# A fused attention, MLP and mixer kernel: later landings in its planner, layer-norm sums as two float32r products, new tables of positions

## Chip, cores and metric

The kernel runs on one core of one Trainium2 chip. The time is that of one execution on the device, in microseconds (us); before the change it is 1037.3 us, the median of three runs (1037.26 to 1037.39). The engines are TensorE (PE in the profile, its weight loads PEld), VectorE (DVE), ScalarE (ACT), GpSimd (POOL) and SyncE (SP), which here only issues transfers.

## The reference

Attention with a causal mask and a bias from a running sum, then a layer norm with an MLP, then a mixing over the sequence with a second MLP:

```python
scores = scale * q @ k.T ; bias = -(cum_i - cum_j)        # per batch and head, S = 576, D = 64
attn = softmax(where(causal, -1e9, scores + min(bias, 0))) ; x = attn @ v   # heads joined: (4, 576, 512)
mu = mean(x, -1) ; var = mean((x - mu) ** 2, -1)
xn = (x - mu) / sqrt(var + 1e-6) * g_ln
x = x + relu(xn @ w_ch1) @ w_ch2                          # 512 -> 2048 -> 512
u = x + (x.T @ U @ V).T                                   # rank 32, over the sequence
out = u + relu(u @ w2_ch1) @ w2_ch2
```

## The kernel before

Four batches of 576 tokens are cut into blocks. In the first layer A0 to A3 are the first 256 tokens of each batch and B0 to B3 the other 320; in the second layer C0 to C3 are the first 512 tokens and T0 the last 64 of all four. Most products are exact to about float32 by splitting both operands into a float32r part and a float32r rest and adding three products (`xh` with `w` high, `xh` with `w` low, `xl` with `w` high, lines 1396 to 1398, 1453 to 1455); C blocks use a scheme with seven sums (lines 1309 to 1311 and 1347 to 1349).

A0 and A1 are normalised token by token (`layer_norm_tok`), with no product. A2, A3 and B0 to B3 are held with features on the partitions, so their mean and variance need a sum over partitions: `ln_sum` adds the four tiles on DVE or POOL into `into` and multiplies the result by a matrix `ones` of 1/512, as one float32 product (line 967). `layer_norm` calls it twice for each block, so there are 12 such sums. What it makes, `xh` and `xl`, is read by the block's first MLP product.

No order is written by hand. Every piece of work is an operation with a priority, a cost per engine it may run on, its reads and writes. `Plan.issue` plans all of them up to five times (`PASSES`), engine by engine, and emits the instructions in the planned order of the shortest plan. So each engine's queue is fixed when the program is built, and each engine takes its queue strictly in order. A transfer (`load`, line 376, loads and stores alike) is taken by the planner to be there 1.5 us (`hop`) after its planned end, plus `lag`. `AT` gives the interval of steps over which a block's attention is spread, `LN` the step at which its layer norm is given, `HEAD` by how much the operations of the start are put ahead of their latest planned time. `split` makes a high part (ACT or DVE) and a rest (DVE or POOL).

Three places matter below. The values of a B block's attention come through two buffers `xs` (line 661), are split into `v` (lines 382, 386) and read much later by line 867; scores come from PE lines 765, 769 and 747 and leave PSUM by DVE lines 773 and 752. In T0 the weights come through two buffers `pB` of 1 MB each (line 1511, `w1_load`), and the second layer's other weights through `w` (line 1517). `t_mix` for T0 loads `t` (line 1161) before its products on line 1244.

Of the kernel before, what the change touches and what calls it, by code (L numbers as in the profile page):

```python
# [10 lines left out]
F32R = mybir.dt.float32r  # L11
I32 = mybir.dt.int32
U32 = mybir.dt.uint32
AF = mybir.ActivationFunctionType
# [17 lines left out]
LAST = ("C0", "C1", "C2", "T0", "C3")  # L32
W2SLOTS = 12

AT = {"A2": (1, 3), "A3": (1, 33), "B0": (26, 49), "B1": (50, 65), "B2": (67, 83), "B3": (83, 100)}
LN = {"A2": 9, "A3": 33, "B0": 62, "B1": 66, "B2": 84, "B3": 102}
W0 = (1, 14)
HEAD = {-100: -1, -50: 127, 1.5: 61, 4.5: 18, -4: 1, -3: -8}
W1 = (16, 60, 59)
PASSES = 4  # L40
AHEAD = 1500


def f(ap):
    return ap.bitcast(F32)


def mm_cost(n):
    return max(106.7, n / 2.4) + 13.3
# [39 lines left out]
class Plan:  # L89
# [196 lines left out]
    def issue(self, warm):  # L286
# [9 lines left out]
        for _ in range(PASSES):  # L296
            prio = self.latest(order, end)
            for o in self.ops:
                prio[o.seq] -= 1e3 * HEAD.get(o.prio, HEAD.get(o.prio + 500, 0))
            use = {e: [0.0] * NW for e in price}  # L300
# [35 lines left out]
def mha_ffn_mixer_ffn(ctx: ExitStack, tc, qkv_p, qkv_a, qkv_b, s, g, w1, w2, U, V, out):  # L336
    nc = tc.nc
    P = Plan(nc)
# [20 lines left out]
    def psum():  # L359
        return P.buf("ps", [128, 512])  # L360
# [6 lines left out]
    def act(prio, n, fn, reads, writes, fixed=94):  # L367
        P.op(prio, {"act": (fixed + 0.8333 * n, fn)}, reads, writes)

    def pe(prio, cost, fn, reads, writes, hold=()):  # L370
        return P.op(prio, {"pe": (cost, fn)}, reads, writes, hold=hold)
# [2 lines left out]
        return 4 * max(n / 2.4, 53.3) + 2.5  # L374

    def load(prio, nbytes, fn, reads, writes, gate=None, rate=350.0, lag=0):
        P.op(prio, {"sp": (475, fn)}, reads, writes, nbytes, gate, rate=rate, lag=lag)

    def copy(prio, n, out, a, reads, writes, psum=False, soft=0.0, slow=False):
        P.op(prio, {  # L380
# [10 lines left out]
    def split(prio, n, hi, lo, src, reads, wh, wl, psum=False, soft=0.0, slow=False):  # L391
        copy(prio, n, hi, src, reads, wh, psum, soft, slow)
        tt(prio, n, lo, src, lambda: f(hi()), ALU.subtract, list(reads) + list(wh), wl, psum, soft)


    def fixed(name, shape, dtype=F32):
        return P.fixed(const.tile(shape, dtype, name=name))

    ident = fixed("ident", [128, 128])
    ones = fixed("ones", [128, 128])  # L400
    eps = fixed("eps", [128, 1])
    odd = fixed("odd", [128, 1])
    g_sb = fixed("g_sb", [128, KT])
    small = fixed("small", [128, 4])
# [14 lines left out]
    PRO = -1e6  # L419

    def setup():
# [14 lines left out]
            dve(PRO, 1, lambda a=a, z=z: nc.vector.memset(odd[a:a + R], z), [], [(odd, "y%d" % a)])  # L436
        dve(PRO, 128, lambda: nc.vector.memset(ones.tile, 1.0 / DM), [], [ones], 0.521)
        P.op(PRO, {"pool": (600, lambda: nc.gpsimd.memset(causal.tile, 0.0))}, [], [causal])
        for y in range(4):
            act(PRO, R, lambda y=y: nc.scalar.activation(sel[R * y:R * (y + 1)], ident[R * y:R * (y + 1), R * y:R * (y + 1)], AF.Copy),  # L440
                [ident, table], [(sel, "y%d" % y)])
# [131 lines left out]
    def w2_ahead(m, gate):  # L573
        prio = NS0 + m - 8
        raw, t = w_raw(prio, 1, m, 1, gate, AHEAD), psum()
        f64_to_f32(prio, 512, lambda: t.tile, lambda: raw.tile, t, raw, psum=True)
# [3 lines left out]
    def w1_ahead(p, gate):  # L580
        prio, dr = NS0 + 2 * p - 9, w1_dr[p]
        raws, ts = [], []
        for z in range(2):
            raw, t = w_raw(prio, 1, 2 * p + z, 0, gate, AHEAD), psum()
            f64_to_f32(prio, 512, lambda t=t: t.tile, lambda raw=raw: raw.tile, t, raw, psum=True)
# [31 lines left out]
    class Pair:  # L617
# [94 lines left out]
        def bias(self, prio, tick, gate):  # L712
# [5 lines left out]
            for y in range(2):  # L718
                load(prio, 256 * S, lambda t=t, y=y: nc.sync.dma_start(
                    t[64 * y:64 * (y + 1)], cum_dr[idx + y:idx + y + 1].to_broadcast([64, S])), [cum_dr], [(t, "y%d" % y)], gate, 260.0, AHEAD // 2)  # L720
                d = lambda y=y: t[64 * y:64 * (y + 1), 512:S]
# [239 lines left out]
    def ln_sum(prio, n, srcs, reads, into):  # L961

        for k in range(1, KT):
            tt(prio, n, lambda: into[:, :n], srcs[0] if k == 1 else lambda: into[:, :n], srcs[k], ALU.add,
               (reads[0] if k == 1 else [into]) + reads[k], [into])
        ps = psum()
        pe(prio - 500, 4 * mm_cost(n), lambda: nc.tensor.matmul(ps[:, :n], ones.tile, into[:, :n], start=True, stop=True), [ones, into], [ps])
        return ps

    def layer_norm(prio, b, blk):  # L970
# [105 lines left out]
    def mix_prep_v(prio, gate):  # L1076
        hi, lo = (P.buf("t", [128, S], F32R) for _ in range(2))
        n = S // 2
        for c0 in (0, n):
            raw, v = P.buf("wr", [128, 1024]), psum()  # L1080
            for z in range(4):
                load(prio, RANK * 8 * n, lambda z=z, c0=c0, raw=raw: nc.sync.dma_start(
                    raw[RANK * z:RANK * (z + 1), :2 * n].bitcast(U32), V[:, c0:c0 + n].bitcast(U32)), [], [(raw, "z%d" % z)], gate, lag=AHEAD)
            f64_to_f32(prio, n, lambda v=v: v[:, :n], lambda raw=raw: raw[:, :2 * n], v, raw, (None, None), psum=True)
# [390 lines left out]
    def put(pos, fn):  # L1475
        plan[int(pos * 4)].append((pos, fn))
# [45 lines left out]
    for st in range(NS0, NS, 2):  # L1522
        _, _, blk, m = steps[st]
# [25 lines left out]
    put(start1 - 12, lambda p, g: mix_prep_v(p, g))  # L1549
    for x in AT:  # L1550
        b, blk = int(x[1]), x[0]
        if x not in FULL:
            for p, pr in enumerate(pairs_of[b, blk]):
                put(max(0, AT[x][0] - 6 + p), lambda p, g, pr=pr: pr.bounce(p, g))
        spread(attn_items(b, blk), *AT[x])
        put(LN[x], lambda p, g, b=b, blk=blk: layer_norm(p, b, blk))
    for (l, b, blk), p in final.items():
# [14 lines left out]


    setup()
    for _, fn in attn_items(0, "A"):
        fn(-100, None)
# [76 lines left out]
```

## Time and profile before

| | |
|---|---|
| median of three runs | 1037.3 us |
| the profiled execution's own time | 1036.19 us |
| its span, first to last instruction | 1034.4 us |
| PE busy | 1017.1 us (98%) |
| DVE busy | 694.6 us (67%) |
| ACT busy | 470.2 us (45%) |
| POOL busy | 138.5 us (13%) |
| DMA engines, main queue | 69.6% |
| granted TensorE clock, mean | 1.000 |

Engine times are sums of what each engine was busy. Products follow each other in a pipeline and are recorded from their start to a modelled end, so a product's recorded duration (308 ns in the mean for the costliest line) is longer than the distance to the next one, and two neighbours overlap. A wait shorter than that overlap doesn't appear as idle time. The 1.8 us between span and time lie outside the first and last instruction.

### The profile page before, as it was taken

The numbers are of one execution on the slowest core, as the hardware profiler recorded it, in microseconds if no ns is written. First come the engines' busy times: TensorE is split into PE (matmuls) and PEld (weight loads), VectorE is DVE, ScalarE is ACT, GpSimd is POOL, SyncE is SP. The second block draws the span as 40 slices with busy tenths as digits, with TensorE's granted clock in tenths as the row PEclk, the third lists the DMA queues.
The fourth block names the chain that finished last, engine by engine and source line by source line (L and its number), as shares of the span: only waits on it lengthen the run. The fifth ranks groups of instructions, "written<-read, shape, count | busy, mean of one in ns | idle before, by whom it ended". The sixth has DMA issues, their size and how long they took to land.

```text
span 1034.4 us, 19312 instructions
## 1 busy us (share of the span) xinstructions
PE 1017.1 (98%) x7110; PEld 938.8 (91%) x7110; DVE 694.6 (67%) x1760; ACT 470.2 (45%) x1104; POOL 138.5 (13%) x288
## 2 busy tenths in 40 slices
PE   8999999999999999989999999999999999999998
PEld 7888888999999999979999999898999899899897
DVE  7999989866988878678754428547446645517444
ACT  6889877755856556557543314312111211112110
POOL 0021333511620222032100000001001000001000
PEclk9999999999999999999999999999999999999999
DMA  8999984668656976595475799981763576487851
GB/s 296 342 339 344 335 310 145 212 228 295 215 165 201 305 245 218 181 315 184 128 286 205 248 394 358 348 321 46 266 217 106 198 240 191 143 287 235 316 172 42
DMA packets 99231, 248.80 MB, mean 241 GB/s; under 512 B 16416, under 2 KB 47392, under 8 KB 94528
## 3 DMA queue, kind: packets, MB, share of 16 engines
q1 hardware_dynamic: 98464, 246.97, 69.6%
q8 instruction: 56, 0.92, 0.4%
q10 hardware_dynamic: 672, 0.59, 0.2%
q14 instruction: 39, 0.32, 0.1%
HBM read 193.97 MB, written 62.99 MB: 248 GB/s over the span
## 4 chain that ended last, share of the span: by engine, by line
PE 77%; DVE 5%; DMA 2%; ACT 2%; issue 1%; SPq 0%; DVEq 0%; POOL 0%; ACTq 0%; POOLq 0%
PE ps L1396 6%; PE ps L1398 5%; PE ps L1397 5%; PE ps L1309 5%; PE ps L1311 5%; PE ps L1310 5%; PE ps L867 4%; PE acc L1453 4%; PE acc L1454 4%; PE acc L1455 4%; PE ps L823 3%; PE acc L1347 3%; PE acc L1349 3%; PE acc L1348 3%; PE ps L1347 3%; PE ps L1348 3%
## 5 line engine op out<-in xcount | busy, mean ns | idle before, releaser
L1396 PE MATMUL ps<-xh,w 128*128 128x256 f32 (+1 forms) x512 | 157.8, 308 | 1.8 <-DVE pB L386 0.9
L1398 PE MATMUL ps<-xl,w 128*128 128x256 f32 (+1 forms) x512 | 151.3, 295 | 0.0
L1397 PE MATMUL ps<-xh,w 128*128 128x256 f32 (+1 forms) x512 | 151.2, 295 | 0.0
L1403 DVE SCALAR_TENSOR_TENSOR hl<-ps,hh 128x256 fp32r<-128x256 f32 (+1 forms) x144 | 64.5, 449 | 94.4 <-ACT hh L1402 94.0
L1402 ACT ACTIVATE hh<-ps 128x256 fp32r<-128x256 f32 (+1 forms) x144 | 58.2, 404 | 119.1 <-PE ps L1398 118.4
L1396 PEld LDWEIGHTS ps<-xh,w 128*128 128x128 f32 x512 | 96.7, 189 | 9.1 <-DVE pB L386 1.6
L1397 PEld LDWEIGHTS ps<-xh,w 128*128 128x128 f32 x512 | 96.8, 189 | 2.2
L1453 PE MATMUL acc<-hh,w 128*128 128x256 f32 (+1 forms) x320 | 97.3, 304 | 0.0
L1398 PEld LDWEIGHTS ps<-xl,w 128*128 128x128 f32 x512 | 96.6, 189 | 0.0
L1454 PE MATMUL acc<-hh,w 128*128 128x256 f32 (+1 forms) x320 | 93.8, 293 | 0.0
L1455 PE MATMUL acc<-hl,w 128*128 128x256 f32 (+1 forms) x320 | 93.8, 293 | 0.0
L1269 ACT ACTIVATE w<-hl 128x256 fp32r<-128x256 f32 x83 | 34.1, 418 | 124.7 <-DVE hl L1289 124.5
L783 ACT ACTIVATE t<-t,mx 128x384 f32<-128x384 f32 (+4 forms) x112 | 68.9, 617 | 47.0 <-DVE mx L773 39.2
L1289 DVE TENSOR_TENSOR hh<-ps,hh 128x256 f32<-128x256 f32 x64 | 27.1, 423 | 77.7 <-ACT hh L381 76.1
L1289 DVE TENSOR_TENSOR hl<-ps,hh 128x256 f32<-128x256 f32 x128 | 48.6, 419 | 44.9 <-PE ps L1311 43.7
L381 ACT ACTIVATE hh<-ps 128x256 f32<-128x256 f32 x31 | 12.0, 386 | 113.9 <-PE ps L1311 113.7
L386 DVE TENSOR_TENSOR pB<-ps,pB 128x384 fp32r<-128x384 f32 (+2 forms) x112 | 60.0, 569 | 5.2 <-ACT pB L381 4.7
L773 DVE CUSTOM_DVE_ANT_0 t<-ps,causal 128x128 f32<-128x128 f32 (+3 forms) x128 | 56.9, 484 | 8.5 <-PE ps L769 8.1
L1453 PEld LDWEIGHTS acc<-hh,w 128*128 128x128 f32 x320 | 60.7, 190 | 1.5 <-issue 1.0
L1454 PEld LDWEIGHTS acc<-hh,w 128*128 128x128 f32 x320 | 60.7, 190 | 0.5
L1455 PEld LDWEIGHTS acc<-hl,w 128*128 128x128 f32 x320 | 60.6, 190 | 0.0
L1295 DVE SCALAR_TENSOR_TENSOR w<-hl,w 128x256 fp32r<-128x256 f32 x128 | 52.3, 426 | 6.6 <-ACT w L1269 5.7
(258 smaller groups left out, 2894.8 us busy)
## 6 DMA issues: line engine op xcount, KB each, us to landing
w<-w_dr SPq DMA_DIRECT2D x112, 512.0 KB, 7.3
pB<-w_dr SPq DMA_DIRECT2D x36, 1024.0 KB, 5.4
qk<-w_dr SPq DMA_DIRECT2D x28, 768.0 KB, 5.2
w_dr<-w SPq DMA_DIRECT2D x32, 512.0 KB, 6.0
w_dr<-wr SPq DMA_DIRECT2D x32, 512.0 KB, 4.8
wr<-w1a SPq DMA_DIRECT2D x16, 512.0 KB, 6.3
wr<-w2a SPq DMA_DIRECT2D x16, 512.0 KB, 6.2
wr<-w1b SPq DMA_DIRECT2D x16, 512.0 KB, 6.5
```

Source lines behind the costliest of these rows:

```text
L386: alts = {"dve": (68 + 1.042 * n, lambda: nc.vector.tensor_tensor(out=out(), in0=a(), in1=b(), op=op))}
L783: act(prio, K, lambda t=t, mx=mx, o=o, K=K, x=x, y=nt * z + x: nc.scalar.activation(t[:, o:o + K], t[:, o:o + K], AF.Exp, bias=mx[:, (1 if ...
L1289: dve(st - 1000, 256, lambda: nc.vector.tensor_tensor(out=d.tile, in0=region(r), in1=a.tile, op=ALU.add), [p, a], [d])
L1347: nc.tensor.matmul(aa[z].tile, w[:, 0, sl], h[:, 0], start=first, stop=False)
L1348: nc.tensor.matmul(aa[z].tile, w[:, 1, sl], h[:, 0], start=False, stop=False)
L1396: nc.tensor.matmul(ps[:, :n], lhs(k, 0), xh[:, k, :n], start=k == 0, stop=False)
L1397: nc.tensor.matmul(ps[:, :n], lhs(k, 1), xh[:, k, :n], start=False, stop=False)
L1398: nc.tensor.matmul(ps[:, :n], lhs(k, 0), xl[:, k, :n], start=False, stop=k == KT - 1)
L1403: dve(st - 1000, n, lambda: nc.vector.scalar_tensor_tensor(out=hl[:, :n], in0=ps[:, :n], scalar=0.0, in1=f(hh[:, :n]), op0=ALU.max, op1=AL ...
L1453: nc.tensor.matmul(a, w[:, 0, sl], hh[:, :n], start=new, stop=False)
L1454: nc.tensor.matmul(a, w[:, 1, sl], hh[:, :n], start=False, stop=False)
L1455: nc.tensor.matmul(a, w[:, 0, sl], hl[:, :n], start=False, stop=last and (z == 1 or blk == "B"))
```

## The change

- `load` lets the planner take every transfer whose priority is above 0 to land at least `LATE` = 1000 ns later than before (an operation that had a larger `lag` keeps it). Only the planned order depends on it; no wait and no transfer is added by it.
- `ln_sum` splits the sum `into` into two float32r tiles from the pool `ls` and multiplies each by a float32r copy `mean_w` of `ones`; one cast at the start makes that copy. In place of one float32 product there are two float32r products, and before them one cast and one subtraction.
- `AT`, `LN` and `HEAD` have new numbers.

```diff
-AT = {"A2": (1, 3), "A3": (1, 33), "B0": (26, 49), "B1": (50, 65), "B2": (67, 83), "B3": (83, 100)}
-LN = {"A2": 9, "A3": 33, "B0": 62, "B1": 66, "B2": 84, "B3": 102}
+AT = {"A2": (1, 3), "A3": (1, 32), "B0": (26, 49), "B1": (50, 65), "B2": (67, 84), "B3": (85, 100)}
+LN = {"A2": 9, "A3": 32, "B0": 62, "B1": 66, "B2": 85, "B3": 102}
-HEAD = {-100: -1, -50: 127, 1.5: 61, 4.5: 18, -4: 1, -3: -8}
+HEAD = {-100: -1, -50: 117, 1.5: 41, 4.5: 16, -4: 1, -3: -8}
+LATE = 1000
...
-        P.op(prio, {"sp": (475, fn)}, reads, writes, nbytes, gate, rate=rate, lag=lag)
+        P.op(prio, {"sp": (475, fn)}, reads, writes, nbytes, gate, rate=rate, lag=max(lag, LATE if prio > 0 else 0))
...
+    mean_w = fixed("mean_w", [128, 128], F32R)
...
+        act(PRO + 1, 128, lambda: nc.scalar.activation(mean_w.tile, ones.tile, AF.Copy), [ones], [mean_w])
...
-        pe(prio - 500, 4 * mm_cost(n), lambda: nc.tensor.matmul(ps[:, :n], ones.tile, into[:, :n], start=True, stop=True), [ones, into], [ps])
+
+        parts = [P.buf("ls", [128, 320], F32R) for _ in range(2)]
+
+        def mm():
+            for z, a in enumerate(parts):
+                nc.tensor.matmul(ps[:, :n], mean_w.tile, a[:, :n], start=z == 0, stop=z == 1)
+
+        split(prio, n, lambda: parts[0][:, :n], lambda: parts[1][:, :n], lambda: into[:, :n], [into], [parts[0]], [parts[1]])
+        pe(prio - 500, 2 * mm_cost(n), mm, [mean_w] + parts, [ps])
```

Since the planner sees other costs and other landings, the order of all five engines is another one from the first pass on. Lines of the changed kernel are numbered 3 to 11 higher. Tile numbers rise with the place in the program's order, so two rows on different engines with near numbers stand near each other.

**A sum of the layer norm, on PE** (A3's first; `ls` holds the sums, `ps` is PSUM). Before:

```order
L747 MATMUL ps3_2636<-qk0_2491 128x288 x3
L747 MATMUL ps4_2645<-qk0_2491 128x288 x3
L967 MATMUL ps2_2653<-ls2_2304,ones_82 128x256
L1396 MATMUL ps5_2595<-xh1_1040,w13_1866 128x256
L1397 MATMUL ps5_2595<-xh1_1040,w13_1866 128x256
```

And in the changed kernel:

```order
L1428 MATMUL acc1_2281<-w11_1904,hl0_2454 128x512
L1429 MATMUL acc1_2281<-w11_1904,hh0_2453 128x512
L975 MATMUL ps4_2715<-ls3_2687,mean_w_84 128x256
L975 MATMUL ps4_2715<-ls1_2696,mean_w_84 128x256
L1407 MATMUL ps0_2720<-xh0_2272,w1_1325 128x256
```

One product became two, of two tiles; both are recorded as 128x256, and the float32 one of before is the one that leaves two records in the trace.

**The values of B3, on DVE** (`xs` are the values as loaded, `v` their split, `t` the scores as they leave PSUM, `xh` and `xl` the result of B2's layer norm). Before, with the second half of the values in the tile `xs0_6726`:

```order
L773 ISA t5_6745,mx3_6769<-ps1_6743,causal_91 128x384
L773 ISA mx3_6769 128x1
L386 TENSOR_TENSOR xc0_6642<-xc0_6642,ls0_6728 128x320
L382 CAST xh0_6801<-xc0_6642 128x320
L382 CAST v0_6710<-xs0_6726 128x5x64
L386 TENSOR_TENSOR xl0_6806<-xc0_6642,xh0_6801 128x320
L386 TENSOR_TENSOR v0_6710<-xs0_6726,v0_6710 128x5x64
L773 ISA t0_6789,mx4_6815<-ps4_6787,causal_91 128x512
L773 ISA mx4_6815 128x1
L773 ISA t1_6790,mx5_6819<-ps1_6788,causal_91 128x512
```

In the changed kernel the second half is in `xs1_6791` and its cast is an instruction of ACT; on DVE:

```order
L776 ISA t0_6814,mx4_6851<-ps1_6812,causal_92 128x512
L776 ISA mx4_6851 128x1
L776 ISA t1_6815,mx5_6861<-ps0_6813,causal_92 128x512
L776 ISA mx5_6861 128x1
L998 TENSOR_SCALAR xc0_6808<-xc0_6808,g_sb_86 128x320
L387 TENSOR_TENSOR ls1_6828<-ls1_6828,ls0_6844 128x320
L383 CAST ls2_6886<-ls1_6828 128x320
L387 TENSOR_TENSOR ls3_6892<-ls1_6828,ls2_6886 128x320
L387 TENSOR_TENSOR v0_6764<-xs1_6791,v0_6764 128x5x64
L755 ISA t2_6824,mx1_6909<-ps2_6839,t2_6824 128x288
```

The scores of the 512-wide tick stood behind the values' second half and stand ahead of it now. On ACT the cast stands behind that tick's two exponentials:

```order
L786 ACTIVATE t0_6814,sm1_6864<-t0_6814,mx4_6851 128x512
L786 ACTIVATE t1_6815,sm1_6864<-t1_6815,mx5_6861 128x512
L997 ACTIVATE xc0_6808<-xc0_6808,g_sb_86 128x320
L382 ACTIVATE v0_6764<-xs1_6791 128x5x64
L1002 ACTIVATE ls0_6921<-ps0_6906,eps_83 128x320
```

The first two rows work on the scores, the fourth is the cast that left DVE.

**Weights for T0, on SP** (`pB` are 1 MB of the first matrix, `w` 512 KB of the second, `out` four stores of 256 KB). Before:

```order
L1511 DMA pB0_11786<-w1_dr5_113 128x2048
L1365 DMA out<-x0_10617 128x512 x2
L1365 DMA out<-x1_10634 128x512 x2
L1517 DMA w1_11844<-w2_dr2_118 128x1024
L1517 DMA w4_11867<-w2_dr3_119 128x1024
L1511 DMA pB1_11878<-w1_dr4_112 128x2048
L1517 DMA w15_11908<-w2_dr0_116 128x1024
L1517 DMA w3_11931<-w2_dr1_117 128x1024
L1511 DMA pB0_11939<-w1_dr3_111 128x2048
```

And in the changed kernel:

```order
L1376 DMA out<-x1_10700 128x512 x2
L1522 DMA pB0_11880<-w1_dr5_114 128x2048
L1528 DMA w9_11912<-w2_dr2_119 128x1024
L1528 DMA w2_11935<-w2_dr3_120 128x1024
L1522 DMA pB1_11943<-w1_dr4_113 128x2048
L1528 DMA w15_11971<-w2_dr0_117 128x1024
L1522 DMA pB0_11993<-w1_dr3_112 128x2048
L1528 DMA w3_12015<-w2_dr1_118 128x1024
```

The weights of the sixth pair of columns (`w1_dr5`) stood ahead of the four stores and stand behind them; one transfer into `w` moved from ahead of `w1_dr3` to behind it. In PE's order 54 products of 128x256 stand between the last one that reads the old tile `pB1_11686` and the first that reads `pB1_11878`; in the changed kernel 66 stand between those of `pB1_11749` and `pB1_11943`, 60 ahead of `pB0_11880` and 66 ahead of `pB0_11993`.

## Rows read from the trace of the kernel before

**Rows 1.** The page's first part: busy us, share of the span, instructions of PE.

```profile
PE 1017.1 (98%) x7110; PEld 938.8 (91%) x7110; DVE 694.6 (67%) x1760; ACT 470.2 (45%) x1104; POOL 138.5 (13%) x288
```

**Rows 2.** Stretches of 25 us; the first line names the columns.

```profile
core 0: us, PE busy (x) PEld busy (x) DVE busy (x) ACT busy (x) POOL busy (x), PEclk, DMA share, GB/s
0.00:25.00 25.00, 21.71 (x174) 17.58 (x176) 18.95 (x74) 17.55 (x41) 2.13 (x12) 1.00 0.88 293
25.00:50.00 25.00, 24.09 (x191) 21.06 (x190) 24.46 (x86) 21.79 (x52) 0.67 (x1) 1.00 0.95 338
...
100.00:125.00 25.00, 23.99 (x162) 20.63 (x160) 22.76 (x56) 20.56 (x50) 5.49 (x9) 1.00 0.98 341
...
250.00:275.00 25.00, 25.00 (x204) 23.28 (x204) 24.84 (x67) 23.00 (x57) 12.26 (x24) 1.00 0.73 240
...
425.00:450.00 25.00, 23.02 (x152) 20.43 (x151) 18.65 (x42) 13.84 (x33) 4.77 (x11) 1.00 0.60 183
450.00:475.00 25.00, 24.06 (x174) 22.41 (x172) 20.87 (x53) 16.35 (x39) 6.77 (x18) 1.00 0.84 275
...
625.00:650.00 25.00, 23.68 (x171) 22.66 (x170) 24.15 (x54) 13.24 (x27) 1.30 (x1) 1.00 0.97 339
...
875.00:900.00 25.00, 24.19 (x155) 21.53 (x154) 15.49 (x38) 4.77 (x11) 0.00 (x0) 1.00 0.41 128
900.00:925.00 25.00, 23.69 (x197) 23.41 (x196) 4.70 (x10) 3.08 (x8) 0.00 (x0) 1.00 0.81 286
...
1025.00:1050.00 25.00, 5.49 (x24) 4.14 (x23) 2.87 (x9) 0.00 (x0) 0.00 (x0) 0.96 0.12 42
```

**Rows 3.** Waits of PE: line, waited for whom: us in total, times, longest.

```profile
PE ps L747 <- DVE mx L773: 2.0, 1, 2.0
...
PE ps L1309 <- DVE x L1463: 1.3, 1, 1.3
PE ps L1396 <- DMA pB<-w_dr: 1.3, 1, 1.3
...
PE ps L1396 <- DVE pB L386: 0.9, 1, 0.9
PE ps L1244 <- DVE t L386: 0.8, 1, 0.8
```

**Rows 4.** Chain that ended last: start us, us, what (sums of 256, then 320 columns).

```profile
169.15 0.43 PE ps L967 x2
169.58 0.12 PE ps L1396
...
248.51 0.54 PE ps L967 x2
...
430.48 0.15 PE ps L1398
```

**Rows 5.** The same chain at B3's values.

```profile
437.59 6.59 DMA xs<-qkv_b
...
444.47 0.49 DVE v L382
...
446.84 0.60 DVE t L773
```

**Rows 6.** The same chain at T0.

```profile
882.05 4.06 DMA t<-t_dr2B
...
906.38 7.61 DMA pB<-w_dr
```

**Rows 7.** Tile `ls`: duration ns min/median/max, first and last start us.

```profile
L386 DVE TENSOR_TENSOR ls<-ls,ls x12: 415/484/492, 167.7 to 536.7; 128x320 f32<-128x320 f32 x11, 128x256 f32<-128x256 f32 x1
...
L388 POOL TENSOR_TENSOR ls<-ls,ls x6: 731/736/883, 123.3 to 250.8; 128x256 f32<-128x256 f32 x5, 128x320 f32<-128x320 f32 x1
...
L996 DVE SCALAR_TENSOR_TENSOR ls<-ls,ls x6: 415/492/1334, 132.3 to 541.0; 128x320 f32<-128x320 f32 x4, 128x256 f32<-128x256 f32 x2
```

## The prediction, made before the changed kernel ran

> **What bounds the kernel now.** I read the engine totals first, then stretches of 25 us, then PE's waits, then the chain that ended last around the longest of them. PE is busy in 1017.1 of a span of 1034.4 us [rows 1], so all that can be gained is PE work taken away and the 17.3 us in which PE idles. The stretches tell where these lie [rows 2]: 4.2 us in the first 50, where the first attention runs ahead of any MLP; 1.0 us from 100 to 125; 2.9 us from 425 to 475; 1.3 us from 625 to 650; 2.1 us from 875 to 925; and 3.9 us at the end, where the last sums and stores run out. That is 15.4 of the 17.3. From 25 to 125 DVE is at 22.8 to 24.5 of 25 us beside PE, so there DVE can hold PE up; later it has slack. PE's waits name the causes [rows 3]: 2.0 us for DVE's score maximum and 0.9 us for a DVE split, both in the stretch 425 to 475; 1.3 us for a transfer into pB and 0.8 us for a split of `t`, both in 875 to 925; 1.3 us for DVE at the change from B3 to C0. The chain shows what stands behind the first two: the transfer of B3's values, 6.59 us from 437.59, for which DVE's cast waits until 444.47; the scores, queued behind the cast, follow at 446.84 [rows 5]. Behind the pB wait stands a transfer of 7.61 us from 906.38, behind the wait for `t` one of 4.06 us [rows 6].
>
> **The sums of the layer norm.** There are 12: four of 256 columns (A2, A3) and eight of 320. One float32 product takes 0.43 us of PE at 256 columns and 0.54 us at 320 [rows 4]. A float32r product takes 0.12 and 0.15 us there [rows 4], two of them 0.24 and 0.30. That is 4 x 0.19 + 8 x 0.24 = 2.7 us of PE, all on PE's path, since PE is the bound wherever the sums run but in 100 to 125 and 425 to 475. There PE could wait longer for what it skips; that concerns A2's and B2's sums, four of the 12, 0.9 us, so the ends are -1.8 and -2.7. I take -2.7.
>
> What is added are 12 casts (six on ACT, six on DVE in the new order) and 12 subtractions (eight more on DVE, four more on POOL). An addition of two such tiles takes 484 ns on DVE and 736 ns on POOL [rows 7]; I use that for all of them. Each sum gets about 1 us later. Who waits for that? `xh` and `xl`, and through them the block's first MLP product. B0's sums stand at 248 us, and PE is busy in 25.00 of 25 us from 250 to 275 while that layer norm runs [rows 2], so nothing waits for it now, and the new order too keeps other blocks' products between the layer norm and its reader. Cost on PE: 0, as long as other blocks' MLP products cover it; without this cover it would be 2 us for each of six blocks, 12 us. The cast that makes `mean_w` falls into the start, before ACT has scores to work on: 0.
>
> **The landings, at B3's values.** Here the order changes as the planner would if it knew of the 6.59 us. Before, the cast of the second half and its subtraction stood on DVE ahead of the scores of the next tick, so one late transfer held the scores, the PSUM tiles they are in, and PE. Now these scores come first, and the cast stands on ACT behind both exponentials. What is late next is PE's product with the values, far behind. I take both waits as gone, -2.9 us (2.0 + 0.9); the ends are 0, if something else in that stretch becomes late by as much, and -2.9.
>
> **The landings, at T0.** Between the last reader of a pB tile and the first of its next content stood 54 products, 54 x 0.12 = 6.5 us, against a transfer of 7.61 us. The difference is the 1.1 us that, with the hand-over, shows as 1.3. Now 66 stand there, 7.9 us: the wait ends. But the tile before it is now loaded behind four stores of 256 KB, with 60 products, 7.2 us, to land in; if it takes the 7.61 us of the row, 0.4 us come back. So -1.0 (from -1.3 to +0.5). For the wait for `t` I take half of its 0.8 us, -0.4 (0 to -0.8): one of its transfers has more work ahead of its reader, the last has not.
>
> At this place the Trainium skill speaks against the change. Its page "DMA: Bandwidth & Descriptors", section "Anatomy of one DMA", gives a transfer a fixed cost of 2.0 us and its bytes at 436 GB/s (a fit of another issuing path than SP's). As an estimate from that page the 1 MB into pB would land in 4.4 us and B3's 160 KB in 2.4 us. Neither could then have made PE wait, to count landings 1 us later would buy nothing, and of the whole sum only the 2.7 us would stay. The trace disagrees, with 7.61 and 6.59 us [rows 5, 6].
>
> **What else the new order does.** All five queues are new, so a wait of the same kind can come up anywhere. Before, PE had four that hang on transfers: 2.0, 1.3, 0.9 and 0.8 us. A plan that takes each landing as 1 us later should keep what exceeds 1 us: 1.0 + 0.3. But intervals and start priorities were moved too, and the planner knows no real queue, so I take +2.0, the longest single wait of before [rows 3]; the ends are 0 and +5, all four again. Start (4.2 us idle), the change from B3 to C0 (1.3) and the end (3.9) I leave as they are. At B3 to C0 the conversion of the last raw weights still stands amid C0's operands on ACT and DVE in both orders. At the start six more fillers stand in the gaps of the first attention; a filler is a 256-column product in time that PE waits through anyway. The ends there are -1.5 and +1.5, a third of what idles.
>
> Sum: -2.7 - 2.9 - 1.0 - 0.4 + 2.0 = -5.0 us. The profiled execution took 1036.2 us, so 1031.2; the median of three runs stands 1.1 us higher, so **1032.3 us**.
>
> **Rivals.** *Only the sums gain.* The waits on transfers move rather than go: PE is so full that a queue which no longer waits at one place meets the next transfer at another. For it speaks that the engine queues are strict and that transfers of 512 KB stand ahead of nearly each small one; against it, that both long waits have a named cause which the new order takes away. Price: -2.7, and new waits of 1.0 us more than the old, 1037.3 - 1.7 = 1035.6, about no change. It is also what the page's rule above gives, with 1034.6.
>
> *DVE's full stretch gets longer* (slower). From 25 to 125 DVE has 0.5 to 2.2 us of slack in 25 [rows 2], and in its last part and just behind it come A2's and A3's four sums: eight more instructions of 0.48 us, 3.9 us, if all fall on DVE. On top a DVE instruction over `ls` that took 492 ns in the median took 1334 once [rows 7]; four such stretches of 0.84 us are 3.4. If all of that reaches PE and the transfers give nothing, 1037.3 - 2.7 + 7.3 = 1041.9. It decides from 4.8 us that reach PE. Against it: DVE has 1697 rows in the new order instead of 1720, for scalings and splits moved to ACT, which has 3 to 5 us of slack there. The skill's "SBUF — State Buffer" has a cause for the long one, under "Reading the diagram": VectorE's instructions with two SBUF inputs and GpSimd's hold one port pair exclusively, and the loser blocks for the whole instruction. The trace agrees for that one instruction only; the median shows no such delay.
>
> *More falls away than I count.* The shorter DVE queue ends the 1.0 us of 100 to 125 and a third of the start, and no new wait comes up: -5.0 - 2.0 - 1.0 - 1.5 = -9.5, 1027.8.
>
> **How the numbers follow.** Forecast 0.50 (1029.5 to 1035); only the sums 0.22 (1034.5 to 1037); DVE's stretch 0.14 (1039.5 to 1043); more falls away 0.14 (1026.5 to 1029.5). Runs of this kernel can tell 0.2%, 2.1 us, from no change: below 1035.2 is faster, above 1039.4 slower. Faster holds the forecast, the last case and a third of the second, 0.50 + 0.14 + 0.08 = 0.72; slower is the DVE case, 0.14; 0.14 is left for the same. The range leaves out the DVE case and the lower edge of the last one: 1028 to 1038.
>
> **What would show it.** Right: two products of 0.12 or 0.15 us for each sum; PE idle under 1 us in the stretch of B3's values, with no cast of `v` on the chain; no wait of PE on pB above 0.5 us; PE's total idle near 14 us instead of 17.3. Wrong: a new wait of PE above 2 us between 50 and 550 us, the chain passing through a cast or subtraction into `ls`, or DVE full from 100 to 175 with PE idle beside it. The forecast falls if PE's idle time isn't below 16 us.

## Result: 1027.1 us, and the profile after

The changed kernel takes 1027.1 us (median of four runs, 1026.3 to 1029.2) beside 1037.35 for the kernel before: a ratio of 0.990, 95% interval 0.989 to 0.992, 10.2 us less. The forecast was 5 us less, 1032.3, with a range that ended at 1028.0. The sign was right, the gain twice as large.

The profiled execution took 1027.39 us, its span is 1025.6. That is 8.8 us below the span of before. The page's first part, against [rows 1]:

```profile
PE 1013.3 (99%) x7116; PEld 938.1 (91%) x7116; DVE 684.2 (67%) x1744; ACT 481.1 (47%) x1136; POOL 151.2 (15%) x297
```

PE's idle time fell from 17.3 to 12.3 us and its busy time by 3.8. Stretches of 25 us, against [rows 2], same columns:

```profile
core 0: us, PE busy (x) PEld busy (x) DVE busy (x) ACT busy (x) POOL busy (x), PEclk, DMA share, GB/s
...
100.00:125.00 25.00, 24.98 (x171) 21.72 (x170) 22.69 (x57) 21.72 (x55) 7.11 (x11) 1.00 0.96 339
425.00:450.00 25.00, 25.00 (x178) 23.89 (x176) 21.15 (x52) 16.63 (x39) 7.03 (x15) 1.00 0.91 292
450.00:475.00 25.00, 24.74 (x175) 23.13 (x174) 20.82 (x50) 17.38 (x40) 8.84 (x18) 1.00 0.68 218
625.00:650.00 25.00, 25.00 (x169) 22.67 (x167) 18.18 (x47) 10.76 (x23) 3.72 (x3) 1.00 0.97 352
875.00:900.00 25.00, 23.79 (x166) 21.98 (x166) 10.35 (x24) 4.06 (x10) 1.29 (x1) 1.00 0.56 197
900.00:925.00 25.00, 24.22 (x204) 24.01 (x203) 4.84 (x11) 3.46 (x9) 0.00 (x0) 1.00 0.81 286
```

PE no longer idles in 100 to 125, 425 to 450 and 625 to 650; from 875 to 925 it idles 2.0 us, as before. PE's waits (line, waited for whom: us, times, longest), against [rows 3]:

```profile
PE ps L768 <- DVE w L387: 2.0, 1, 2.0
PE acc L1614 <- DVE ones L439: 1.5, 1, 1.5
PE ps L1407 <- ACT wr L382: 1.0, 1, 1.0
PE ps L1407 <- DMA pB<-w_dr: 0.8, 1, 0.8
```

The first two lie in the start; the 2.0 is 0.6 and 0.8 in two further traces of the changed kernel. The waits at B3's values and at the change from B3 to C0 are gone; the one on pB is 0.8 instead of 1.3, and a new one of 1.0 us stands in T0 on a cast of `wr`.

To see where the time went I compared the two traces by work: when has PE finished the same amount of products (sums of the layer norm and fillers not counted, each product weighed by its pitch)? The difference of these times is the lead of one kernel over the other. Of after over before, by stretches of before's time:

| us of before | to 52 | 52-165 | 165-300 | 300-425 | 425-475 | 475-630 | 630-655 | 655-885 | 885-960 | all |
|---|---|---|---|---|---|---|---|---|---|---|
| what is there | start | A2, A3 | B0 | B1 | B2's sums, B3's values | B3 | change to C0 | | T0 | |
| lead won | -0.3 | +3.2 | +0.7 | +1.0 | +3.8 | +0.4 | +1.5 | 0.0 | -1.1 | +9.1 |

The chips on which the experiments ran executed the kernel before in 1033.0 to 1041.4 us, so a median there is good to about 1 us, and the intervals of the ratios are 2 to 5 us wide. The two further traces of the changed kernel gave the same leads to within 0.9 us in each stretch behind the start (the start +0.2 and +0.8 instead of -0.3). So I read the places from traces and the sums of them from times.

### The profile page after: what moved, and what is told of

Its sections match the earlier page's. It is cut to its first block, busy times and chain, and to the rows that moved or that the text cites. A ratio compares the mean times of both kernels' runs of the same rounds, so it can differ in the third digit from the quotient of the medians.

```text
span 1025.6 us, 19424 instructions
## 1 busy us (share of the span) xinstructions
PE 1013.3 (99%) x7116; PEld 938.1 (91%) x7116; DVE 684.2 (67%) x1744; ACT 481.1 (47%) x1136; POOL 151.2 (15%) x297
## 4 chain that ended last, share of the span: by engine, by line
PE 87%; DVE 6%; DMA 4%; ACT 1%; issue 1%; SPq 1%; POOL 0%; DVEq 0%; ACTq 0%; POOLq 0%
PE ps L1407 7%; PE ps L1409 7%; PE ps L1408 7%; PE ps L1320 5%; PE ps L1322 5%; PE ps L1321 5%; PE ps L870 4%; PE acc L1464 4%; PE acc L1465 3%; PE acc L1466 3%; PE ps L826 3%; PE acc L1360 3%; PE acc L1358 3%; PE acc L1359 3%; PE ps L1358 3%; PE ps L1359 3%
## 5 line engine op out<-in xcount | busy, mean ns | idle before, releaser
L382 ACT ACTIVATE hh<-ps 128x256 f32<-128x256 f32 x32 | 12.3, 385 | 114.2 <-PE ps L1322 114.2
L776 DVE CUSTOM_DVE_ANT_0 t<-ps,causal 128x256 f32<-128x256 f32 (+3 forms) x128 | 56.5, 484 | 5.5 <-PE ps L772 5.0
L382 ACT ACTIVATE pB<-ps 128x512 fp32r<-128x512 f32 (+3 forms) x103 | 48.6, 517 | 18.7 <-PE ps L826 18.7
```

The costliest lines, as they stand in the source:

```text
L382: "act": ((51 if psum else 94) + 0.8333 * n, lambda: nc.scalar.activation(out(), a(), AF.Copy)),
```

## The experiments

### One term each, with the order kept

These keep the planned order of one kernel and change what is emitted, so nothing else moves.

**The sums alone, in before's order.** The last bits are dropped, so no cast is needed.

```diff
-        pe(prio - 500, 4 * mm_cost(n), lambda: nc.tensor.matmul(ps[:, :n], ones.tile, into[:, :n], start=True, stop=True), [ones, into], [ps])
+        def mm():
+            for z in range(2):
+                nc.tensor.matmul(ps[:, :n], mean_w.tile, into[:, :n], start=z == 0, stop=z == 1)
+
+        pe(prio - 500, 4 * mm_cost(n), mm, [ones, into], [ps])
```

> The order of before, kept as it is; each of the 12 sums becomes two float32r products of the same sum, whose last bits are left out (it is rounded to float32r as it is added up, so no cast and no subtraction is needed). The steps of the prediction: four sums at 0.24 for 0.43 us and eight at 0.30 for 0.54 us, all on PE's path, -2.7 us: 1034.6. Rival, part is absorbed: in the stretches 100 to 125 and 425 to 475 PE then waits longer for what it skips, -1.8 us: 1035.5. Rival, the sums are worth more than their rows: PE's busy time fell by 3.8 us from before to after, and if all of it is theirs, 1033.5.

Ratio 0.9996 (0.998 to 1.0012): -0.4 us, between -2.1 and +1.2. By time -2.7 and -3.8 fail, and -1.8, the rival with a part absorbed, lies just inside the interval. By trace each of the eight wide sums gave 0.23 to 0.25 us at its place; of A2's and A3's, what is won (0.19 at a time) is lost again within 15 us, as that rival has it. All that was gained, and more, went at one other place, 4.3 us at 345 to 354 us. The chain there, and PE's longest wait (the other 1.7 of its 4.3 us is the one of [rows 5]):

```profile
337.99 4.81 DMA xs<-qkv_b
...
345.78 0.15 POOL xs L668
...
345.95 0.49 DVE v L382
346.44 0.80 DVE xl L386
347.23 1.06 DVE v L386
```

```profile
PE ps L752 <- DVE mx L778: 4.3, 2, 2.6
```

It is the pattern of [rows 5] at another block: the values' cast stands on DVE ahead of the scores and waits for a transfer (by way of POOL's padding of `xs`), and the scores wait behind. In the profile of before this place just holds. Then the clock fell (columns as above, stretches of 1 us):

```profile
346.00:347.00 1.00, 0.35 (x3) 0.09 (x1) 1.00 (x2) 0.00 (x0) 1.00 (x3) 1.00 1.02 418
347.00:348.00 1.00, 0.00 (x0) 0.00 (x0) 1.00 (x2) 0.00 (x0) 0.95 (x1) 1.00 1.01 414
348.00:349.00 1.00, 0.04 (x1) 0.04 (x1) 1.00 (x4) 0.06 (x1) 0.00 (x0) 1.00 1.11 379
349.00:350.00 1.00, 1.00 (x7) 1.00 (x8) 1.00 (x5) 1.00 (x4) 0.26 (x2) 1.00 1.03 203
350.00:351.00 1.00, 1.00 (x7) 1.00 (x6) 0.84 (x3) 1.00 (x4) 0.31 (x2) 0.70 1.02 238
351.00:352.00 1.00, 1.00 (x6) 1.00 (x5) 0.84 (x3) 1.00 (x3) 0.12 (x1) 0.50 0.98 330
352.00:353.00 1.00, 1.00 (x6) 1.00 (x5) 0.51 (x2) 1.00 (x2) 0.00 (x0) 0.50 1.04 272
353.00:354.00 1.00, 1.00 (x6) 1.00 (x6) 0.93 (x2) 0.23 (x2) 0.47 (x2) 0.60 0.86 200
```

After a wait of 2.6 us PE ran at the lower level (0.50, that is 1.2 of 2.4 GHz) until 354: 0.30 + 0.50 + 0.50 + 0.40 = 1.7 us of products lost. So the wait cost 4.3 us, not 2.6.

**The sums made dearer, in after's order.**

```diff
-                nc.tensor.matmul(ps[:, :n], mean_w.tile, a[:, :n], start=z == 0, stop=z == 1)
+                nc.tensor.matmul(ps[:, :n], ones.tile, f(a[:, :n]), start=z == 0, stop=z == 1)
```

> The changed kernel with its order kept; only the type of the 24 products of the sums is changed, each is a float32 product of the same tile: 0.86 and 1.08 us for a sum instead of 0.24 and 0.30. If a microsecond of PE in the sums is a microsecond of the end, as the prediction has it: 4 x 0.62 + 8 x 0.78 = 8.7 us more, 1035.8. If waits elsewhere take up a third or more of it, below 1033.

Ratio 0.9969 (0.9958 to 0.998), 1034.1 us: 6 to 8.5 more than two later runs of the changed kernel (0.9887 and 0.991, each beside its own runs of before). By trace it falls back by 0.77 to 0.79 us at each of the eight wide sums, against 0.78, and by 0.4 to 0.6 at three places around A2's and A3's, against 0.62. So at the eight wide sums a microsecond of PE is a microsecond of the end, and the price of the rows holds; at A2's and A3's half to two thirds of it arrive.

**The values of B3 alone, in before's order.** Operations 2605 and 2606 are the cast and the subtraction, 2717 is the split behind both scores.

```diff
+        late = [c for c in best if c[0].seq in (2605, 2606)]
+        best = [c for c in best if c[0].seq not in (2605, 2606)]
+        at = 1 + next(n for n, c in enumerate(best) if c[0].seq == 2717)
+        best[at:at] = late
```

> The order of before, kept as it is but for one cast and one subtraction on DVE, those of B3's values that waited for the transfer of 6.59 us: they move behind the two scores of the 512-wide tick and the split behind these. The steps of the prediction: the waits of 2.0 us (L747 for the maximum) and 0.9 us (L1396 for a split into pB) both go, -2.9 us: 1034.4. Rival, only the first goes with it, the second has another cause: -2.0, 1035.3. Rival, the wait moves to the product with the values or to another late transfer: 1036.3 or more.

Ratio 0.999 (0.9976 to 1.0004): -1.0 us, +0.4 to -2.5. By trace it wins 2.5 us at 449 us and gives back 0.75 at 455; in 425 to 475 the lead grows by 1.7. PE's waits there:

```profile
PE ps L827 <- ACT t L802: 1.3, 1, 1.3
PE ps L1400 <- DVE pB L390: 0.5, 1, 0.5
```

The 2.0 us are gone and the 0.9 is 0.5, but, as the last rival has it, PE meets the next late thing of that order, a scaling on ACT, at 1.3. Its profiled execution also lost 1.5 us between 300 and 425 us, ahead of the edit, so the time says little here.

**Work added on DVE, in after's order.** Every tenth DVE operation of a stretch is followed by an addition that nobody reads.

```diff
+            if e == "dve" and EXTRA[0] <= s < EXTRA[1]:
+                seen += 1
+                if seen % EXTRA[2] == 0:
+                    self.nc.vector.tensor_tensor(out=self.spare, in0=self.ones, in1=self.ones, op=ALU.add)
```

> The changed kernel with its order kept, and 21 more additions of 128x128 on DVE between about 57 and 160 us, some 0.2 us each, 4 us in all; nobody reads them. If DVE sets the pace there, so that the work that the new plan took off it (25.0 - 22.2 us idle instead of 1.0 in the 25 us from 50) is what PE gained, PE's lead over the same kernel without them falls by 2 us or more by 165 us: 1029 or more. The prediction left this stretch at 0, as if PE alone set the pace there: then under 1 us.

> The same with 19 such additions between about 250 and 350 us, where DVE is less full. If the pace of DVE counts only from 57 to 160 us: under 1 us by 350 us, 1027 to 1028. If it counts wherever attention runs: as much as in the other kernel.

Ratios 0.9915 (0.9899 to 0.9932) and 0.991 (0.9895 to 0.9925), the changed kernel beside them 0.9887. The tile's rows (duration ns min/median/max) in the first and the second:

```profile
L338 DVE TENSOR_TENSOR spare<-ones x21: 254/281/612, 60.5 to 156.0; 128x128 f32<-128x128 f32 x21
```

```profile
L338 DVE TENSOR_TENSOR spare<-ones x19: 264/283/529, 252.4 to 348.6; 128x128 f32<-128x128 f32 x19
```

They are 0.28 us, not 0.2. Beside the three traces of the changed kernel, 5.9 us in the first kernel cost 1.2 to 2.0 us of lead between 55 and 165, and 5.4 us in the second cost 1.6 between 280 and 350. DVE counts there, by a fifth to a third of its time, and no more in the first stretch than in the second. My theory that the early stretch is special fell. With it falls a reading of the prediction, that DVE has slack behind 125 us: [rows 2] has DVE at 24.84 of 25 us from 250 to 275.

### One part of the change each, planned anew

The parts are the hunks of the diff above: S the sums, L the line with LATE, T the tables.

```diff
 e1 = before + S      e2 = before + L      e3 = before + T
 e4 = after - L       e5 = after - S       e6 = after - T
```

> The kernel before with the new sums alone, the order planned anew. The steps of the prediction: 1034.6, and the wait at B3's values stays. Theory, the sums also bring the 2.2 us of 54 to 165 us (fewer instructions on DVE in the new plan): gain of about 3 us by 165 us, 1032.4. Rival, a plan made anew for another reason moves waits at random: anything from 1033 to 1041, with waits of over 2 us at new places.

> The kernel before with LATE = 1000 alone; old sums, old tables, the order planned anew. The steps of the prediction: the landings carry B3's values and T0 and the new waits, -2.9 - 1.4 + 2.0 = -2.3 us: 1035.0, with the wait of 2.0 us at B3's values gone. Rival, LATE carries all that the sums don't, -10.2 + 2.7 = -7.5 us: 1029.8. Rival, the tables carry it and LATE alone only shuffles waits: within 1 us of 1037.3.

> The kernel before with the new AT, LN and HEAD alone. In the profiles of before and after the place at which the changed kernel gains more than was forecast is 54 to 165 us, where DVE is nearly full: 3.0 us there, 0.8 of them the sums of A2 and A3. Theory, the tables do it (A3's layer norm a step earlier, another start): gain of 2 us or more by 165 us, nothing at B3's values, 1035 or less. Rival, the landings or the sums do it, or it needs them together: no gain by 165 us, 1037.

> The changed kernel without LATE: sums and tables. The landings' share as the prediction has it is -2.9 - 1.4 + 2.0 = -2.3, as the profiles have it -3.1 at B3's values, -1.5 at the change from B3 to C0 and +1.2 at T0 = -3.4. Without it: 1027.1 + 2.3 = 1029.4 or 1027.1 + 3.4 = 1030.5, with a wait of 2 us or more between 425 and 475 us. Rival, LATE carries more, because the other parts work only with it: 1033 or more.

> The changed kernel with the old sums: LATE and tables, float32 products of 0.43 and 0.54 us. The sums' share as the prediction has it is -2.7: 1029.8, with the gain by 165 us less only by the 0.8 us of A2's and A3's sums. Rival, the sums' share is larger, since the new plan took work off DVE: 1032 or more, and no gain by 165 us.

> The changed kernel with the old AT, LN and HEAD: sums and LATE. Theory from the runs so far: the wait at B3's values goes in every plan made anew, the gain of 1.5 us at the change from B3 to C0 comes with LATE, and only LATE and the tables together lose nothing between 54 and 430 us. Then this kernel gains at B3 and at C0 but loses 2 to 5 us before 430 us: 1031 to 1034. Rival, LATE with the sums is enough and the tables are without effect: within 1.5 us of the changed kernel.

> The changed kernel itself, beside the kernel before on the chip that runs the experiments, as their baseline: 10.2 us less than before. In the profiles the single terms of this sum are: start +0.2, 54 to 165 us -3.0, 165 to 430 -1.5, B3's values -3.7, B3's sums -0.5, change from B3 to C0 -1.5, T0 +1.2, with the sums of the layer norm in the second to the fifth term.

The ratio to before with its interval, what it makes of 1037.3 us, the lead won over before by places, and PE's idle time from 165 to 300 us (135 us less its busy time):

| kernel | ratio (95%) | us | 52-165 | 165-300 | 300-425 | 425-475 | 630-655 | 885-960 | idle 165-300 |
|---|---|---|---|---|---|---|---|---|---|
| before | | | | | | | | | 0.4 |
| T | 1.0 (0.9985-1.0015) | 0.0 | +1.7 | -4.4 | -1.1 | +2.7 | -0.2 | 0.0 | 2.5 |
| S | 0.9964 (0.9952-0.9977) | -3.7 | +0.4 | -3.1 | -1.3 | +3.6 | -0.2 | +0.6 | 2.3 |
| S+T | 0.9975 (0.9964-0.9986) | -2.6 | +1.2 | -3.3 | -2.7 | +4.5 | -0.2 | +0.9 | 2.7 |
| L | 0.9977 (0.9963-0.999) | -2.4 | -0.3 | -1.3 | +0.2 | +4.3 | +1.5 | +0.6 | 0.2 |
| L+T | 0.9949 (0.993-0.9968) | -5.3 | +2.2 | -0.8 | -0.2 | +3.5 | +1.5 | -1.6 | 0.2 |
| L+S | 0.9907 (0.9889-0.9926) | -9.6 | +3.5 | +0.3 | -1.1 | +5.2 | +0.9 | -0.1 | 0.1 |
| L+S+T, again | 0.9887 (0.9869-0.9905) | -11.7 | +2.8 | +0.7 | +1.1 | +3.4 | +1.5 | -1.3 | 0.0 |

- *B3's values* (425 to 475): 2.7 us or more in every new plan, with the landings counted later or not. The wait belonged to one order, and each of these plans loses it (T has another one of 1.3 us there, for a sum). The theory that LATE takes it away fell.
- *165 to 300*: without LATE three of three plans have 2.3 to 2.7 us of idle time, where before has 0.4; with it none has more than 0.2. The stretch of S+T, and the chain behind its longest wait, of 2.1 us:

```profile
165.00:300.00 135.00, 132.31 (x1060) 125.36 (x1059) 106.10 (x274) 92.27 (x218) 48.91 (x95) 1.00 0.67 222
```

```profile
163.54 7.24 DMA xs<-qkv_b
170.78 0.05 issue
170.83 0.14 POOL xs L665
170.98 0.69 POOL ls L388
171.66 0.04 issue
171.71 0.39 PE ps L974
```

  POOL's padding of B's values waits for a transfer of 7.24 us, the addition of the layer norm's sum stands behind it on POOL, and PE waits for that sum. In the plans of S and of T a transfer `qk<-qkvB` of 4.52 and 6.71 us stands on the chain ahead of one of their waits. With LATE and the same sums, the row of L+S is

```profile
165.00:300.00 135.00, 134.94 (x1093) 128.56 (x1094) 112.16 (x286) 94.67 (x222) 46.24 (x92) 1.00 0.65 215
```

- *The change to C0*: 0.9 to 1.5 us with LATE; none without, where two waits of 0.8 us in all stand in place of the one of 1.3.
- *T0*: with LATE -1.6 to +0.6, without 0.0 to +0.9: the landings bring nothing there.
- *The tables*: L+S without them is as fast as the whole change within the intervals; T alone gains nothing. The theory that LATE needs the tables to lose nothing before 430 us fell: by time -9.6 beside -11.7, with intervals that overlap, and by trace L+S stands 2.7 us ahead in 52 to 425.
- *The parts do not add up*: L and S alone give -2.4 and -3.7, together -9.6. B3's wait, which each of them takes away, counts only once (5.2 instead of 4.3 + 3.6), but in 52 to 425 us L+S stands 2.7 us ahead of before, where L loses 1.4 and S 4.0.
- *The expectations*: L's -2.4 is the -2.3 of the steps by luck, since it is made of +4.3 at B3's values and +1.5 at C0, with 1.9 lost in the start and 1.4 from 52 to 425. T's and S+T's times are those of the last rivals (1037; 1033 or more), T's with +1.7 in 52 to 165 us that are lost again behind it. S's time does not decide between its three, but the wait at B3 went, 0.4 us and not 3 were won by 165, and no wait above 2 us came. L+T (1032.0) is above the 1029.8 of the sums' price, yet keeps its gain by 165 us, so neither theory holds whole.

### Other amounts for the landings

```diff
-LATE = 1000
+LATE = 500
```

and 2000.

> The changed kernel with LATE = 500. If the landings act by their amount: part of the effect, between the kernel without LATE (about 1034.5) and the changed one (1027), PE idle of 0.5 to 2 us between 165 and 300 us, near 1030. Rival, one lucky plan: no order in the amounts, anything from 1026 to 1036.

> The changed kernel with LATE = 2000. If the landings act by their amount and 1000 is enough: no PE idle between 165 and 300 us, no wait at the change from B3 to C0, 1026 to 1029; T0 loses as with 1000. Rival, one lucky plan: anything from 1026 to 1036, with PE idle of 2 us or more between 165 and 300 us.

500: ratio 0.9974 (0.996 to 0.9988), -2.7 us; 0.6 us idle from 165 to 300, but two waits of 3.0 us in all for a score maximum, the longer one until 373, the clock at the lower level behind them, and 4.1 us lost from 300 to 425. 2000: ratio 1.0072 (1.0056 to 1.0087), 7.5 us *slower* than before and outside what either expectation had:

```profile
165.00:300.00 135.00, 127.67 (x979) 117.97 (x977) 108.72 (x286) 90.01 (x212) 44.97 (x92) 0.96 0.64 207
```

PE idles 7.3 us there, and in two pieces of 190 to 215 us the clock falls; some 14 us of lead are lost in these 25 us. So there is no order in the amounts: 0, 500, 1000 and 2000 give 1034.7, 1034.6, about 1027 and 1044.8. The theory that LATE works by its amount fell, with 2000 most clearly; what it gives with 1000 is a plan in which behind the start no wait above 0.5 us comes up in the first layer. By time the changed kernel and, within the intervals, L+S are the fastest of the nine new plans here, which run from 11.7 us faster than before to 7.5 slower.

### T0's last mixer product

```diff
+        best = move((4313, 4314), (0, 4370))
+        best = move((4372, 4374, 4373, 4375), (1, 4336))
```

Operation 4314 is the mixer product and 4313 the subtraction on POOL ahead of it; 4370 is the second last of C2's products, 4372 to 4375 C2's last two additions and stores, 4336 the last split behind the mixer product. In the first version 4313 was not moved, so the product multiplied by a rest of `t` that was not yet written; that time is a hint only.

> The changed kernel with its order kept but for T0's last mixer product (eight products on PE, the addition and the splits behind it on DVE and ACT), which moves ahead of the last six products of C2, and C2's last two additions into the output, which move behind those splits. If the loss at T0 comes from this product standing directly ahead of its reader: the waits of 1.0 (ACT wr) and 0.25 us (DVE wr) go, -1.2 us, and with them the lower clock behind these waits in the executions that have it: 1025.9 beside 1027.1. Rival, what comes later (the transfers into pB behind four stores) takes it back: within 0.4 us by 955 us.

> The changed kernel with its order kept but for T0's last mixer product and POOL's subtraction ahead of it, which move ahead of the last six products of C2, and C2's last two additions into the output, which move behind the splits of that product's result. The subtraction ends at 884.15 us of the changed kernel's profile, the six products start at 884.04, so PE should hardly wait for it. If the loss at T0 comes from the product's place: the waits of 1.0 and 0.25 us go, 1.2 us less than the changed kernel beside it. Rival, as in the run before: a wait of about 0.9 us stays, since the chain behind the product (addition, cast, subtraction) is longer than the six products, and 0.3 to 0.8 us are gained by 955 us.

> The changed kernel itself, beside the other one: 10 to 12 us less than before.

In the changed kernel, PE's rows with an idle time ahead (in brackets, us and what ended it):

```profile
887.35 0.39 PE L1407 MATMUL ps<-wr,pB 128*128 128x256 f32 x1 [0.96 <-ACT wr L382]
...
888.10 0.39 PE L1409 MATMUL ps<-wr,pB 128*128 128x256 f32 x1 [0.25 <-DVE wr L387]
...
915.32 0.39 PE L1407 MATMUL ps<-wr,pB 128*128 128x256 f32 x1 [0.78 <-DMA pB<-w_dr]
...
939.03 0.39 PE L1320 MATMUL ps<-xl,qk 128*128 128x256 f32 x1 [0.16 <-ACT xl L382]
...
939.90 0.39 PE L1322 MATMUL ps<-xl,qk 128*128 128x256 f32 x1 [0.37 <-DVE xl L387]
```

The first version took 0.9899 (0.9882 to 0.9917) of before; a wait of 0.9 us for DVE's `wr` stayed. The second has these waits from 880 to 955 us:

```profile
PE ps L1415 <- DMA pB<-w_dr: 0.6, 1, 0.6
PE ps L1330 <- DVE xl L395: 0.4, 1, 0.4
PE ps L1328 <- ACT xl L390: 0.2, 1, 0.2
PE ps L1263 <- POOL t L397: 0.2, 1, 0.2
```

Both waits on `wr` are gone, 0.2 us for POOL came, and 1.0 us of lead over the changed kernel is won at the product's place and kept to the end; T0 now costs nothing against before (+0.1). By time: 1025.6 us beside 1027.4 for the changed kernel on the same chip, ratios to before 0.9897 (0.9873 to 0.9921) and 0.991 (0.9887 to 0.9934), which do not tell the two apart. Nor is its trace the shortest: its span is 1025.5 us beside 1025.6, since its start came out 0.5 us worse, and L+S has 1024.4.

## Why the prediction was right and wrong

The step that failed is the fifth term of the sum, "what else the new order does". It put +2.0 us of new waits there, and 52 to 165 us and the change from B3 to C0 at nothing. The plan that was built has no new wait above 0.5 us behind the start but at T0 (0.6 in one of its three traces), and it gained about 2.5 and 1.5 us at those two places: some 6 us better than that term. T0, forecast at -1.4, came out at +1.1 to +1.6 and took nearly half of them back. Of the 5.2 us between forecast and result the traces show about 4, a gain of 8.8 to 9.1 us where the sum has 5.0; the rest lies between single executions and medians (the profiled execution of before stood 1.2 us below its median, that of the changed kernel 0.2 above).

| step | forecast | measured |
|---|---|---|
| sums | -2.7 | eight times 0.23 to 0.25; A2's and A3's not seen in one order, half to two thirds in the other: -1.9 to -2.4 |
| B3's values | -2.9 | -2.5 to -3.3 in three traces, 425 to 475 without B2's two sums (0.5) |
| T0 | -1.4 | +1.1 to +1.6 |
| new waits elsewhere | +2.0 | none above 0.5 outside T0 and the start |
| 52 to 165, "DVE's full stretch" | 0 | about -2.5 (3.2 with up to four sums of 0.19) |
| change from B3 to C0 | 0 | -1.5 |
| start, end | 0 | -0.8 to +0.3, differs between executions |

**The sums** were right for the eight wide ones, 1.9 of the 2.7 us; what A2's and A3's are worth hung on the order, as the forecast's lower end had it. The rows of the finished product are those of the forecast:

```profile
174.93 0.23 PE ps L975 x2
...
245.95 0.29 PE ps L975 x2
```

The casts and subtractions cost PE nothing in this order, as forecast: it idles 0.02 us at most ahead of any of these products. DVE has 684.2 us of work instead of 694.6.

**B3's values** were right in size by luck and wrong in cause. I argued that the planner puts the scores first because it counts the 6.59 us as later. But in every new plan, with LATE or without, PE no longer waits there for the cast's sake. The wait was a property of the old plan, and moving the cast alone in that plan gave 1.7 us, not 2.9.

**T0** failed, in sign too. Both waits did end at the places that I priced, for some 1.5 us of lead each. The transfer behind the four stores took 4.97 us and the one with 66 products ahead of its reader 6.02, and PE waited for neither. But waits came at three places that I had not priced. On the cast and subtraction of `wr`, behind the product of which `t` is an operand, PE waits 0.96 and 0.25 us (some 2.1 us of lead): in the new order nothing stands between that product and its reader. Two transfers later PE waits 0.78 us (1.0 of lead; not in the trace in which the clock fell), where 60 products, 7.0 us, stand against a transfer of 7.81:

```profile
907.47 7.81 DMA pB<-w_dr
```

For `xl` PE waits 0.16 and 0.37 us at 939 us (1.1 of lead), in all three traces. I counted three transfers into pB and the transfers ahead of the mixer product, and not the later transfers or the chain behind the product.

**The new waits**, +2.0, lay near what new plans do: three of them without LATE have 2.3 to 2.7 us in 165 to 300 us alone. The plan that was built has none there. That and the change to C0, and not B3 or T0, are what came with LATE here, and 500 and 2000 show that it is no rule.

**52 to 165** was the rival "more falls away", with its place right and its size half. I read one stretch of it, the 1.0 us of 100 to 125 [rows 2], and left it at 0. PE's idle time in the whole of 52 to 165 was 113.0 - 110.9 = 2.1 us and is 0.1:

```profile
52.00:165.00 113.00, 110.92 (x789) 96.92 (x790) 103.16 (x278) 93.33 (x251) 30.29 (x62) 1.00 0.91 320
```

```profile
52.00:165.00 113.00, 112.92 (x811) 99.02 (x810) 102.35 (x282) 91.84 (x251) 31.43 (x59) 1.00 0.90 323
```

"A shorter DVE queue" does not explain it: DVE has 102.4 us of work there instead of 103.2, and by the experiment with added work 0.8 us are worth 0.2 to 0.3 on PE. Which order of which instructions gives the rest is open. No part has it to itself: T alone gives +1.7, L+T +2.2 with the old sums, L+S +3.5, and the sums' own share of the latter is 0.6 to 0.8.

**The change to C0** went with LATE in the plans with 1000. I had seen that the conversion of raw weights stands amid C0's operands in both orders and taken that as enough. DVE's last addition into `x` ahead of C0's product comes 14.9 us after its first one for C0 in before (639.02 after 624.08) and 12.3 us after in the changed kernel (628.52 after 616.22). Why the planner does that with LATE was not tried.

By these rows the rival that was most nearly right is the third, 1027.8; it had 0.14. It was right that no new wait came up ahead of T0. That its sum fits to 0.7 us is luck: it counts -1.4 at T0 and -1.5 in the start, which did not come, and not the change to C0. Nor does a plan without new waits in 165 to 300 have to gain in 52 to 165: L has none and stands at -0.3.

The Trainium skill's rule that spoke against the change ("DMA: Bandwidth & Descriptors", "Anatomy of one DMA") gives, as an estimate from its figures, 2.4 us for B's values. In two of the waits shown above they took 7.24 and 4.81 us, and there the trace disagrees again. These are long ones: the median of the 32 transfers of that size is 4.0 us in before and 3.0 in the changed kernel. What such waits cost hung on the order, not on the landing alone.

## What to carry to other kernels

When a change makes a planner order everything anew, a single wait of the old order can go by that alone, whatever the change was for. B3's did so in all nine new plans, while the one at C0 shrank only to 0.8 us in the three without LATE. What decides is which waits the new order has, and neighbouring settings (500, 1000, 2000) can differ by 17 us. Price such a change in two parts. The first is what it does in a frozen order, which rows of the trace give to a tenth of a microsecond at the place itself, though the frozen order may meet its next late transfer behind it. The second is a spread for the new plan: the nine here lie between 11.7 us faster and 7.5 slower than before, 2.7 faster in the middle. To find causes, compare traces by work done and keep the order while one term is changed.

## Unexpected of the hardware

A wait of PE can cost more than its length. Behind waits of 2.6 us (the sums in before's order, until 349), 2.2 (S+T, 375) and 2.1 (LATE = 500, 373) the granted clock stood at the lower level for some 3 us, which cost 1.7 us more in the case shown above; behind 2.1 us at 172 in S+T and the 2.0 us of [rows 3] it did not. Behind the 0.96 and 0.25 us at T0 it did so in some executions and not in others. In the kernel with dearer sums:

```profile
891.00:892.00 1.00, 0.44 (x4) 0.33 (x3) 0.84 (x3) 0.07 (x1) 0.00 (x0) 1.00 0.96 363
892.00:893.00 1.00, 0.50 (x2) 0.30 (x2) 1.00 (x4) 0.66 (x2) 0.00 (x0) 1.00 0.96 377
893.00:894.00 1.00, 0.85 (x4) 0.85 (x5) 0.77 (x3) 0.00 (x0) 0.00 (x0) 0.65 0.04 12
894.00:895.00 1.00, 1.00 (x7) 1.00 (x6) 0.00 (x0) 0.00 (x0) 0.00 (x0) 0.50 0.00 0
895.00:896.00 1.00, 1.00 (x7) 1.00 (x7) 0.00 (x0) 0.00 (x0) 0.00 (x0) 0.50 0.06 16
896.00:897.00 1.00, 1.00 (x7) 1.00 (x7) 0.00 (x0) 0.13 (x1) 0.00 (x0) 0.65 0.00 0
```

PE was busy 0.94 us of two, and 0.35 + 0.50 + 0.50 + 0.35 = 1.7 us went. In two of the three traces of the changed kernel the clock stayed at 1.00 there, in the third it fell. It may be part of why its single runs differ by 3 us and more; that was not tried.

And the subtractions on DVE that take 0.48 us in the median [rows 7] took 0.80 and 1.06 us in the first experiment's chain, in the two microseconds (346 to 348) in which POOL is busy 1.00 and 0.95. The prediction had the cause from the Trainium skill ("SBUF — State Buffer", "Reading the diagram": VectorE with two SBUF inputs and GpSimd shut each other out for a whole instruction) and called it a single case; here the long subtractions lie inside a wait of PE. They do so in B3's wait of before too, where the two at 444.88 and 445.70 took 0.90 and 1.14 us while POOL worked: of what held the scores there, about 1.1 us is their excess over 0.48 us and not the transfer. In all 19 traces the 614 additions and subtractions on DVE of 128x320 in SBUF that no POOL instruction overlaps took 0.47 to 0.50 us; of the 354 that one overlaps, 68 took more than 0.6. So the rows of every order agree with POOL as the cause, though it was not tried by itself.
